# Routing arithmetic kept in tokens, and the order of all steps written out as a list, in a fused linear attention and mixture-of-experts kernel

## The chip, the cores and the metric

The kernel runs on one core of a Trainium2 chip. The metric is the device time of one execution in microseconds (us). Before the change the median of three runs is 667.26 us (663.68, 667.26 and 671.38). TensorE is called PE here, VectorE DVE, ScalarE ACT, GpSimd POOL and SyncE SP.

## The reference

Attention with random features over eight batches and eight heads gives 4608 rows of 512; each row then goes through one of eight experts, the one with the largest gate logit.

```python
# q, k, v: [8, 8, 576, 64]; omega: [128, 64]
def phi(x):
    proj = np.einsum('bhsd,md->bhsm', x, omega)
    h = proj - np.sum(x * x, axis=-1, keepdims=True) / 2.0
    h = h - np.max(h, axis=-1, keepdims=True)
    return np.exp(h) / np.sqrt(m)
q_p, k_p = phi(q_s), phi(k_s)                     # q, k scaled by 64 ** -0.25
kv = np.einsum('bhsm,bhsd->bhmd', k_p, v)
z = np.sum(k_p, axis=2)
num = np.einsum('bhsm,bhmd->bhsd', q_p, kv)
den = np.einsum('bhsm,bhm->bhs', q_p, z)[..., None] + 1e-06
x = (num / den) -> rows [4608, 512]

logits = x @ w_gate                               # [4608, 8]
e_idx = np.argmax(logits, axis=1)
gate_w = softmax(logits)[np.arange(N), e_idx]
eom = 1.0 / (1.0 + np.exp(-(x @ w_output_gate)))
for e in range(8):
    mask = e_idx == e
    h = np.maximum(x[mask] @ w1[e], 0.0)          # w1[e]: [512, 1024]
    out[mask] = gate_w[mask, None] * eom[mask, e, None] * (h @ w2[e])
```

## The kernel before

**Attention.** The work is cut into 32 units: four groups of tokens (nine chunks of 128 tokens each) by eight pieces of heads. A unit u goes through these steps, each named by its kind and its unit:

- SP loads k and q in two layouts (ld t, ld n) and v (ld v), ahead of time.
- ACT makes the f16 part of the transposed input (hi, tile xhi) and the squares (sqa, tile sqt, L442); POOL makes the remainder (lo, tile xlo, L436).
- PE multiplies by omega (pp, L502). DVE takes the maximum (L524) and makes the bias (nb, L537); ACT takes the exponential (ex, tile ef, L543).
- ACT casts ef to f16 (eh, tile es, L564), POOL makes the remainder beside it (el, L566). PE sums es times v (kv, L639), DVE scales the sum (kvs, L700).
- PE makes the gate products of the kv sums (kt, and kg at L682, in f32).
- For most units SP transposes es by a DMA from SBUF to SBUF (eT, tile et, L620); the first eight units are transposed on PE. PE multiplies et by kvs (pn, L713); DVE normalizes (tiles xf and xh), POOL makes the remainder xl (L747), and SP stores the rows to DRAM (rows).

Buffers limit how far units run apart: es, et and the input tiles have two each.

**Routing.** After the eight units of a group, DVE finds the expert of every token: route makes the one-hot r_one of the argmax; PE's counts multiplies it with a triangle of ones, which gives each token its place within its expert; ranks, places, table, assign and lists on DVE turn that into lists of 128 tokens; PE (pid) and DVE then give the indices gi. All this is a chain of small DVE instructions on a tile called rt, with 8 or 9 elements per partition in most. Experts are filled in blocks of 128 tokens: the arithmetic turns a count into blocks by a cast to int32, a shift by 7 and a cast back.

**Experts.** Item n is one block of up to 128 tokens of one expert. There are 49 slots in groups of 8, 8, 9 and 24; with these inputs 38 run. POOL gathers the rows (gx, L1446); SP transposes them (xt, L1458); PE multiplies by w1 (hA and hB, L1483, in f16 with a remainder w1l); ACT takes the relu (hh, L1490), DVE its remainder (rest, tile hl, L1494); PE multiplies by w2 (out, L1514; L1506 where at most 64 rows are filled); ACT scales the result (os, L1567); POOL scatters it (put, L1556). When the expert changes, SP brings the weights, ACT cuts them to f16 (sw, L364, w1h and w2h) and DVE makes the remainders (swl, L368). The items of group 0 stand among the units of the later groups; the items of the last group come after all units.

**The order of all this.** Every step is added to a `Plan` with its engine, a cost, what it follows, the tiles that it reads, and the PSUM banks that it takes and frees. `Plan.order` is a list scheduler: it picks, at each moment of a modelled time, the step with the lowest rank among those that could start now. The rank is a due time plus a number for the kind of step (`SHIFT`):

```python
s = dict(..., rank=(rank + SHIFT.get(key[0], 0.0), self.seq), bank=bank)
...
k = min((k for k in ready if steps[k]["est"] <= best + TIE), key=lambda k: steps[k]["rank"])
```

The steps are issued in the order that comes out, on each engine's queue; five banks are kept for one class of requests, three for another (`Plan({"a": 5, "b": 3})`). There are 3333 steps.

Of the kernel before, what the change touches and what calls it, by code (L numbers as in the profile page):

```python
# [21 lines left out]
P = 128  # L22
# [4 lines left out]
NSC = 4  # L27
# [4 lines left out]
KEY = 64  # L32
KC = DM // P
# [39 lines left out]
SHIFT = {'hi': -1.4, 'lo': 0.3, 'sqa': 1.9, 'sqr': 2.3, 'T': 1.8, 'pp': 0.1, 'mx': 0.5, 'nb': -0.4, 'ex': -2.0, 'eh': -0.7, 'el': 1.4, 'eT': 0.4, 'kv': -0.5, 'kvs': -1.6, 'pn': -0.1, 'xf': -0.9, 'xh': 0.1, 'xl': 0.7, 'xT': -3.4, 'rows': -0.1, 'lg': -2.2, 'lga': -1.4, 'route': -1.8, 'gx': 1.7, 'xt': 1.0, 'hA': 0.7, 'hB': -1.1, 'relu': -2.1, 'rest': -0.6, 'out': 0.3, 'os': -0.1, 'put': 1.0}  # L73
# [25 lines left out]
C_END = C_DOWN + 1  # L99


def constants():
# [6 lines left out]
    c[:, C_ITEM:C_PART] = np.arange(NITEM)  # L109
# [4 lines left out]
    c[FEW:, C_DOWN] = -float(FEW)  # L114
    c[:, C_BOTH + 1 : C_UPPER : 2] = np.arange(NSC * NC) * P
# [3 lines left out]
    m[:, 2, :] = np.arange(P)  # L119
    m[:, 3, :] = np.eye(P)  # L120
    return c, m, np.eye(P, dtype=np.float32)


class Plan:

    HANDOFF, DRAIN, DMA_START, DMA_END, DMA_TURN, BACKLOG, LATE = 0.19, 0.13, 0.65, 0.95, 0.3, 2.5, 2.5
    TICK, ENOUGH = 3.413, 3060.0

    def __init__(self, banks):
        self.steps, self.seq, self.banks, self.bank_of = {}, 0, banks, {}
        self.part = 0
        self.makers, self.readers, self.bufs = {}, {}, {}

    def add(
        self, key, engine, cost, fn, after=(), rank=0.0, tiles=(), bank=None, frees=(), dma=0.0, turn=False, early=None, cols=None,
        lead={},
    ):


        assert key not in self.steps, key
        cost = cost if isinstance(cost, tuple) else (cost,) * len(engine)
        bank = [] if bank is None else bank if isinstance(bank, list) else [bank]
        s = dict(key=key, eng=engine, cost=cost, fn=fn, after=list(after), rank=(rank + SHIFT.get(key[0], 0.0), self.seq), bank=bank)  # L150
        s.update(frees=frees, dma=dma, turn=turn, tiles=sorted(set(tiles)), early=early, part=self.part, lead=lead)
        s["cols"] = cost[0] * 2400.0 if cols is None else cols
        self.seq += 1
        self.steps[key] = s
        for tag, i in s["tiles"]:
            self.readers.setdefault((tag, i), []).append(key)
# [18 lines left out]
    def lag(self, a, b):  # L175

        if a == b:
            return 0.0 if a == ("PE",) else self.DRAIN
        return 0.06 if b == ("SP",) else self.HANDOFF

    def order(self):
        steps = self.steps
        users, missing = {}, {}
        for k, s in steps.items():
            deps = set(s["after"])
            for tag, i in s["tiles"]:
                deps |= set(self.readers.get((tag, i - self.bufs[tag]), ()))
            s["deps"] = deps
            missing[k] = len(deps)
            for d in deps:  # L190
                assert d in steps, (k, d)
                users.setdefault(d, []).append(k)
        free_at = {"SP": 0.6, "DVE": 0.9, "POOL": 0.7, "ACT": 1.9, "PE": 0.1}
        bank_free = {b: 0.0 for b in range(sum(self.banks.values()))}
        bank_cls, b0 = {}, 0
        for c, n in self.banks.items():
            bank_cls[c] = range(b0, b0 + n)
            b0 += n
        bank_cls["e"] = range(b0)
        dma_free = 0.0  # L200
        ready = {k for k in steps if not missing[k]}
        at = {k: 0.0 for k in ready}
        out, done = [], {}
        busy = {}
        while ready:
            best = None
            for k in ready:
                s = steps[k]
                engs = s["eng"]
                t = max([at[k]] + [free_at.get(e, 0.0) for e in engs])  # L210
                if s["bank"]:
                    free = sorted(bank_free[b] for b in bank_cls[s["bank"][0][0]] if b in bank_free)
                    t = max(t, free[len(s["bank"]) - 1] if len(free) >= len(s["bank"]) else 1e9)
                if s["dma"] and engs == ("SP",):
                    t = max(t, dma_free - self.BACKLOG)
                s["est"] = t
                if best is None or t < best:
                    best = t
            assert best < 1e9, sorted(ready, key=str)[:20]

            k = min((k for k in ready if steps[k]["est"] <= best + TIE), key=lambda k: steps[k]["rank"])
            s = steps[k]
            t = s["est"]
            ready.remove(k)
            for cls, name, _ in s["bank"]:
                b = min((b for b in bank_cls[cls] if b in bank_free), key=lambda b: bank_free[b])
                del bank_free[b]
                self.bank_of[name] = b
            if s["eng"] == ("PE",):

                end, left = t, s["cost"][0]
                while left > 1e-6:
                    tick = int(end / self.TICK + 1e-6)
                    speed = 1.0 if busy.get(tick - 1, 0.0) >= self.ENOUGH else 0.5
                    part = min(left, ((tick + 1) * self.TICK - end) * speed)
                    busy[tick] = busy.get(tick, 0.0) + s["cols"] * part / s["cost"][0]
                    end, left = end + part / speed, left - part
                free_at["PE"] = end
            else:
                end = t + max(s["cost"])  # L240
                for e, cost in zip(s["eng"], s["cost"]):
                    free_at[e] = t + cost
            for name in s["frees"]:
                bank_free[self.bank_of[name]] = end + self.HANDOFF
            fin = end if s["early"] is None else t + s["early"]
            if s["dma"]:
                b = max(end + self.DMA_START, dma_free)
                dma_free = b + s["dma"] + (self.DMA_TURN if s["turn"] else 0.0)

                fin = b + s["dma"] + self.DMA_END + (self.LATE if s["turn"] else 0.0)  # L250
            done[k] = fin
            s["t"] = (t, end, fin)
            out.append(s)
            for u in users.get(k, ()):
                missing[u] -= 1
                e = fin + self.lag(s["eng"], steps[u]["eng"]) - steps[u]["lead"].get(k, 0.0)
                at[u] = max(at.get(u, 0.0), e)
                if not missing[u]:
                    ready.add(u)
# [1398 lines left out]
```

## Time and profile before

| | |
|---|---|
| median of the three runs | 667.26 us (663.68 to 671.38) |
| profiled execution, its own time | 664.8 us |
| its span in the trace | 663.0 us |
| mean granted clock of PE | 0.961 of full speed |
| DMA moved | 129.09 MB |
| last product of PE ends | 649.8 us after the span's start |

The profile comes from one execution. Its page gives the busy time of each engine, in all and in 40 equal slices of the span as tenths, and below them the granted clock of PE. Rows of groups give one line, engine, operation and tile; the count after x, the busy time, the mean of one in ns, and the idle time ahead of them with the releaser that ended most of it. Rows of the timeline give start, duration, engine, line, operation, output tile <- input tiles, shapes, and in square brackets the wait ahead of the instruction and what ended it. In the waits of an engine the three numbers are the time in all, the count and the longest.

### The profile page before, as it was taken

Reading aid. Unit: us, or ns where it says so; the run is one execution under the profiler, and the core shown is the slowest. Engines: PE = TensorE matmul, PEld = TensorE weight load, DVE = VectorE, ACT = ScalarE, POOL = GpSimd, SP = SyncE. Lnnn points to the kernel's source line nnn. Section 1 sums busy time; section 2 is a strip of 40 time slices with the busy share of each in tenths; the row PEclk is TensorE's granted clock in tenths of the full one; section 3 lists DMA queues with packets and bytes.
Section 4 is the critical chain, followed back from the end, with each engine's and each line's share of the span. In section 5 each row is a group of like instructions: output and inputs, shape, how many; then the busy total and the mean of one; then the engine's idle time right before and its main releaser. Section 6 shows DMA issues by size and latency. Waiting matters only on the chain. (4 is left out here: it accounts for less than half of the span.)

```text
span 663.0 us, 22360 instructions
## 1 busy us (share of the span) xinstructions
PE 610.9 (92%) x8732; PEld 479.8 (72%) x8732; DVE 425.7 (64%) x1277; ACT 413.0 (62%) x970; POOL 340.5 (51%) x235
## 2 busy tenths in 40 slices
PE   6999987799999899999788999999999899999972
PEld 6899976677777677777555777878677767676761
DVE  4899889876978897576587776753882611431160
ACT  5876887589989759898575588762611611521150
POOL 1342445569957958989376588965031312131110
PEclk9999977699999999999899999999999999999996
DMA  9544578997999979999999675877747647642730
GB/s 317 207 136 129 174 281 197 254 252 167 319 275 287 272 191 221 227 225 235 277 257 170 149 194 126 144 134 198 226 113 211 183 92 234 172 90 62 268 112 8
DMA packets 145895, 129.09 MB, mean 195 GB/s; under 512 B 104271, under 2 KB 127441, under 8 KB 144465
## 3 DMA queue, kind: packets, MB, share of 16 engines
q1 hardware_dynamic: 139760, 107.45, 64.0%
q0 software_dynamic: 5984, 19.72, 9.4%
q8 instruction: 85, 1.39, 0.9%
q14 instruction: 66, 0.53, 0.3%
HBM read 83.86 MB, written 19.30 MB: 156 GB/s over the span
## 5 line engine op out<-in xcount | busy, mean ns | idle before, releaser
L1483 PE MATMUL ph<-xt,w1h 128*128 128x128 f16 (+1 forms) x2432 | 205.2, 218 | 3.4 <-ACT os L1567 1.6
L1483 PE MATMUL ph<-xt,w1l 128*128 128x128 f16 (+1 forms) x1216 | 201.3, 218 | 0.0
L1483 PEld LDWEIGHTS <-w1h 128*128 128x128 f16 x2432 | 181.9, 98 | 10.8 <-issue 4.4
L543 ACT ACTIVATE ef<-pp,nb 128x128 f32<-128x128 f32 x576 | 162.8, 392 | 41.5 <-DVE nb L537 31.6
L1494 DVE SCALAR_TENSOR_TENSOR hl<-ph,hh 128x512 f16<-128x512 f32 (+1 forms) x76 | 50.6, 666 | 116.4 <-ACTq L1412 76.6
L566 POOL TENSOR_TENSOR es<-ef,es 128x1152 f16<-128x1152 f32 x44 | 104.9, 2391 | 35.6 <-ACT es L564 19.5
L524 DVE TENSOR_REDUCE pp<-pp 128x3 f32<-128x384 f32 x192 | 102.8, 557 | 28.2 <-PE pp L502 27.7
L1483 PEld LDWEIGHTS <-w1l 128*128 128x128 f16 x1216 | 118.5, 98 | 0.3 <-DVEq L1407 0.2
L1446 POOL DMA_INDIRECT gx<-rows,gi x38 | 40.8, 1074 | 140.5 <-ACT os L1567 100.6
L1514 PE MATMUL po<-w2h,hl 128*128 128x512 f16 x280 | 107.0, 382 | 2.4 <-DVEq L1412 1.5
L1514 PE MATMUL po<-w2h,hh 128*128 128x512 f16 x280 | 107.4, 384 | 0.0
L1514 PE MATMUL po<-w2l,hh 128*128 128x512 f16 x280 | 107.1, 383 | 0.0
L1490 ACT ACTIVATE hh<-ph 128x512 f16<-128x512 f32 (+1 forms) x76 | 44.3, 583 | 80.0 <-PE ph L1483 73.6
L1514 PEld LDWEIGHTS <-hh 128*128 128x128 f16 x560 | 51.9, 99 | 58.0 <-issue 3.7
L1567 ACT ACTIVATE os<-po,gx 128x512 f32<-128x512 f32 (+1 forms) x38 | 25.5, 670 | 72.9 <-PE po L1514 68.0
L436 POOL TENSOR_TENSOR xlo<-xt,xhi 128x1152 f16<-128x1152 f32 x24 | 57.2, 2382 | 13.2 <-ACT xhi L429 12.7
L713 PE MATMUL pn<-kvs,et 128*128 128x81 f16 (+1 forms) x960 | 48.2, 210 | 12.3 <-DMA et<-es 7.2
L713 PEld LDWEIGHTS <-et 128*128 128x128 f16 (+1 forms) x960 | 41.6, 105 | 21.2 <-DMA et<-es 7.9
L564 ACT CAST es<-ef 128x1152 f16<-128x1152 f32 x44 | 51.3, 1176 | 7.4 <-DMA et<-es 6.9
L1514 PEld LDWEIGHTS <-hl 128*128 128x128 f16 x280 | 27.6, 99 | 35.3 <-DVE hl L1494 1.3
L502 PE MATMUL pp<-omh,xhi 64*128 64x128 f16 x432 | 43.0, 223 | 5.0 <-DVE xf L726 2.7
L747 POOL TENSOR_TENSOR xs<-xf,xs 128x576 f16<-128x576 f32 x32 | 42.1, 1317 | 8.9 <-DVE xs L743 8.1
(183 smaller groups left out, 1052.8 us busy)
## 6 DMA issues: line engine op xcount, KB each, us to landing
r<-w SPq DMA_DIRECT2D x10, 2048.0 KB, 11.9
xt<-kqt SPq DMA_DIRECT2D x32, 576.0 KB, 4.7
xn<-kqn SPq DMA_DIRECT2D x24, 576.0 KB, 4.9
rawv<-v SPq DMA_DIRECT2D x32, 325.0 KB, 3.7
rows<-xs SPq DMA_DIRECT2D x16, 576.0 KB, 5.3
r<-w SPq DMA_DIRECT2D x8, 512.0 KB, 6.6
ef<-w SPq DMA_DIRECT2D x2, 512.0 KB, 4.4
et<-w SPq DMA_DIRECT2D x2, 512.0 KB
```

The costliest lines, as they stand in the source:

```text
L436: lambda t0=t0, t1=t1: nc.gpsimd.tensor_tensor(out=xl(u)[:, t0:t1], in0=xt32(u)[:, t0:t1], in1=xh(u)[:, t0:t1], op=ALU.subtract),
L502: nc.tensor.matmul(banks["pp", 2 * u + i, g][:, c, :], x[r, t], w[r, :], start=(a == 0), stop=(a == len(ops) - 1))
L524: nc.vector.tensor_reduce(out=pp[:, 3, 0:3], in_=pp[:, 0:3, :], op=ALU.min, axis=AX.X)
L543: nc.scalar.activation(ef(n)[:, c, :], banks["pp", n, g][:, c % 3, :], AF.Exp, bias=nb(n)[:, c : c + 1], scale=-SK)
L564: nc.scalar.copy(es(slot_es(n))[:, 0], ef(n))
L566: nc.gpsimd.tensor_tensor(out=es(slot_es(n))[:, 1], in0=ef(n), in1=es(slot_es(n))[:, 0], op=ALU.subtract)
L713: nc.tensor.matmul(pn[lo:hi, c - c0, :], a[:, c, lo:hi], w[:, b, :], start=(i == 0), stop=(i == len(ops) - 1))
L747: nc.gpsimd.tensor_tensor(out=x[:, :, P + o : P + o + D], in0=xf(u)[:, :, 0:D], in1=x[:, :, o : o + D], op=ALU.subtract)
L1483: nc.tensor.matmul(ph[:, f4, 0:w_], w[qd][:, kk, fo : fo + P], xt(n)[:, x, 0:w_], start=(a == 0), stop=(a == 3 * KC - 1))
L1490: nc.scalar.activation(hh(n)[:, sl, 0:w_], banks["ph", n, g][:, :, 0:w_], AF.Relu)
L1494: nc.vector.scalar_tensor_tensor(out=hl(n)[:, sl, 0:w_], in0=banks["ph", n, g][:, :, 0:w_], scalar=0.0, in1=hh(n)[:, sl, 0:w_], op0=ALU.ma ...
L1514: nc.tensor.matmul(po, x(n)[:, f, :], w[f // 2][:, f % 2, :], start=(f == 0 and a == 0), stop=(f == FC - 1 and a == 2))
```

## The change

Two things are changed.

**First, the routing keeps its counts in tokens.** The state `cnt` and `done`, the item numbers and the block starts are multiples of 128 where they were block numbers. A count is rounded to whole blocks by adding a constant ROUND, 1.5 x 2^23 x 128, and taking it off again: at that size an f32 has steps of 128. A count is held lower by 63.5 so that this rounds down. The running count is added by PE: counts begins its two sums with a product of the f32 identity and `cnt`. The steps fall from 9 to 7 in table (8 in the last group), from 8 to 7 in assign, from 4 to 3 in ranks, from 5 to 3 in places; the copy of the chunk numbers (cp) moves from lists to places in the first three groups. In all 23 DVE steps fewer, six in each of groups 0 to 2 and five in group 3, and eight PE products more.

**Second, the order is written out.** `Plan` has no scheduler any more. `ORDER` lists the numbers of all 3310 steps (numbered as they are added), and `BANKS` has one digit for each request of a bank; any of the eight banks may serve any request.

```diff
+MIDDLE = (P - 1) / 2
+ROUND = 1.5 * 2.0**23 * P
...
+ORDER = """
+0 31 32 4 86 3 7 33 5 35 34 36 16 1 2 28 88 37 6 39 40 48 49 41 50 8 38 42 43 51 52 54 45 55 57 89 44 53 56 10 139 19
...
+BANKS = """
+0123456701235467150234671234507631276415702361546734052671364127056341263471652037120476153472365031042635612702067431
...
     def order(self):
...
+        numbered = list(self.steps.values())
+        out = [numbered[int(x)] for x in ORDER.split()]
...
-    plan = Plan({"a": 5, "b": 3})
+    plan = Plan()
...
     def first_state():
-        nc.vector.tensor_scalar(cnt, eidx, float(KEY * P), None, ALU.mult)
-        nc.vector.tensor_scalar(done[:, 0, :], eidx, float(KEY), None, ALU.mult)
-        nc.vector.tensor_copy(done[:, 1, :], eidx)
+        nc.vector.tensor_scalar(cnt, eidx, float(KEY * P), -MIDDLE, ALU.mult, ALU.add)
+        nc.vector.tensor_scalar(done, eidx, float(KEY * P), ROUND, ALU.mult, ALU.add)
...
     def counts(j):
...
-        nc.tensor.matmul(pos[:, 0:NC, :], tri, one, start=True, stop=False)
+        nc.tensor.matmul(pos[:, 0:NC, :], ident, cnt.unsqueeze(1).broadcast_to([P, NC, NE]), start=True, stop=False)
+        nc.tensor.matmul(pos[:, 0:NC, :], tri, one, start=False, stop=False)
...
+        nc.tensor.matmul(pos[:, NC, :], ident, cnt, start=True, stop=False)
         for c in range(NC):
-            nc.tensor.matmul(pos[:, NC, :], ones, one[:, c, :], start=(c == 0), stop=(c == NC - 1))
+            nc.tensor.matmul(pos[:, NC, :], ones, one[:, c, :], start=False, stop=(c == NC - 1))
 
     def ranks(j):
...
-        nc.vector.tensor_tensor(
-            out=pk, in0=pos[:, 0:NC, :], in1=cnt.unsqueeze(1).broadcast_to([P, NC, NE]), op=ALU.add
-        )
-        yield
-        nc.vector.tensor_tensor(out=cnt, in0=cnt, in1=pos[:, NC, :], op=ALU.add)
-        yield
-        nc.vector.tensor_tensor(out=pk, in0=pk, in1=rt[j]["one"], op=ALU.mult)
+        nc.vector.tensor_tensor(out=pk, in0=pos[:, 0:NC, :], in1=rt[j]["one"], op=ALU.mult)
+        yield
+        nc.vector.tensor_copy(cnt, pos[:, NC, :])
...
     def places(j):
...
-        nc.vector.tensor_copy(ri, rank)
-        yield
-        nc.vector.tensor_scalar(ri, ri, 7, None, ALU.arith_shift_right)
-        yield
-        nc.vector.tensor_copy(key, ri)
-        yield
-        nc.vector.scalar_tensor_tensor(out=rank, in0=key, scalar=-float(P), in1=rank, op0=ALU.mult, op1=ALU.add)
+        nc.vector.tensor_scalar(key, rank, ROUND, ROUND, ALU.add, ALU.subtract)
+        yield
+        nc.vector.tensor_tensor(out=rank, in0=rank, in1=key, op=ALU.subtract)
...
     def table(g):
...
-        nc.vector.tensor_scalar(av_i, cnt, float(P - 1) if g == NG - 1 else 0.0, None, ALU.add)
-        yield
-        nc.vector.tensor_scalar(av_i, av_i, 7, None, ALU.arith_shift_right)
...
-        nc.vector.tensor_tensor(out=av, in0=av_i, in1=done[:, 0, :], op=ALU.subtract)
...
-        nc.vector.tensor_tensor(out=t["av"], in0=av_i, in1=done[:, 0, :], op=ALU.subtract)
+            for x in (av, t["av"]):
+                nc.vector.scalar_tensor_tensor(out=x, in0=cnt, scalar=ROUND, in1=done, op0=ALU.add, op1=ALU.subtract)
```

The lists differ from what the scheduler gave in many places: 84 of PE's 502 steps, 692 of DVE's, 341 of ACT's, 104 of POOL's and 144 of SP's stand elsewhere. Three places follow. In them L922 to L958 of the kernel before are L979 to L1021 of the changed one; in general the line numbers of the changed kernel are some 56 to 60 higher.

On DVE, in the routing of group 0, places (writing keys) and table (writing r_avs) run side by side, with pieces of the next units (nb, pp) between. Before:

```order
L922 CAST rt_1670<-rt_1670 128x9
L947 TENSOR_SCALAR rt_1670<-cnt 128x8
L537 SCALAR_TENSOR_TENSOR nb_1783<-pp_0_1561,sqs_1553 128x3
L924 TENSOR_SCALAR rt_1670<-rt_1670 128x9
L949 TENSOR_SCALAR rt_1670<-rt_1670 128x8
L926 CAST keys<-rt_1670 128x9
L952 TENSOR_TENSOR rt_1670<-rt_1670,done 128x8
L928 SCALAR_TENSOR_TENSOR rt_1670<-keys,rt_1670 128x9
L955 TENSOR_TENSOR r_avs<-rt_1670,done 128x8
L930 TENSOR_TENSOR place<-cmt,rt_1670 128x1152
L958 TENSOR_TENSOR rt_1670<-ahead,rt_1670 128x64
```

The same place of the changed kernel:

```order
L1012 SCALAR_TENSOR_TENSOR rt_1656<-cnt,done 128x8
L1012 SCALAR_TENSOR_TENSOR r_avs<-cnt,done 128x8
L590 SCALAR_TENSOR_TENSOR pp_1_1671<-pp_1_1671,sqs_1512 128x3
L979 COPY rt_1656<-cft 128x18
L1015 TENSOR_TENSOR rt_1656<-ahead,rt_1656 128x64
L594 SCALAR_TENSOR_TENSOR nb_1780<-pp_1_1671,sqs_1512 128x3
L581 TENSOR_REDUCE pp_2_1691<-pp_2_1691 128x3
L1018 TENSOR_REDUCE r_tot<-rt_1656 128x1
L981 TENSOR_SCALAR keys<-rt_1656 128x9
L1021 TENSOR_REDUCE rt_1656<-rt_1656 128x8
L590 SCALAR_TENSOR_TENSOR pp_2_1691<-pp_2_1691,sqs_1512 128x3
L983 TENSOR_TENSOR rt_1656<-rt_1656,keys 128x9
```

The four steps of table up to r_avs have become two, the chunk copy stands here, and table now runs ahead of places, whose wide product (place, 128x1152) comes later.

On ACT, between the squares of a later unit (sqt) and the relu of item 11 (hh), stand the f16 cast of unit 23 (es, which needs an es buffer that the et transfer of unit 21 must have read) and the cutting of item 12's w1 (w1h, inside a branch that is taken only when the expert changes). Before:

```order
L442 ACTIVATE sqt_7209<-xn_6621 128x1152
L564 CAST es_7216<-ef_6867 128x1152
L1407 COMPARE_AND_BRANCH
L364 ACTIVATE w1h_90<-r_106 128x1024
L364 ACTIVATE w1h_91<-r_106 128x1024
L364 ACTIVATE w1h_92<-r_106 128x1024
L364 ACTIVATE w1h_93<-r_106 128x1024
L1407 UNCONDITIONAL_BRANCH x2
L1392 UNCONDITIONAL_BRANCH
L1490 ACTIVATE hh_7154<-ph_1_7156 128x512
```

The same place of the changed kernel:

```order
L499 ACTIVATE sqt_7175<-xn_6534 128x1152
L600 ACTIVATE ef_7093<-pp_1_7100,nb_7085 128x128 x3
L1463 COMPARE_AND_BRANCH
L421 ACTIVATE w1h_90<-r_106 128x1024
L421 ACTIVATE w1h_91<-r_106 128x1024
L421 ACTIVATE w1h_92<-r_106 128x1024
L421 ACTIVATE w1h_93<-r_106 128x1024
L1463 UNCONDITIONAL_BRANCH x2
L1448 UNCONDITIONAL_BRANCH
L621 CAST es_7198<-ef_6839 128x1152
L1546 ACTIVATE hh_7122<-ph_1_7126 128x512
```

The cutting of w1 now stands ahead of the cast, with three exponentials of a later unit ahead of both. On PE at the same place the order was hB 11, both halves of pn 22 (which waits for et), out 11 and hA 12; it is now hB 11, out 11, half of kv 23, both halves of pn 22 and hA 12. On ACT the cutting of item 12's w2 moves ahead of the scaling (os) of item 11 and of the copy of kv (kvf).

On POOL, in the time of group 1's counts, the remainder el of unit 17 (es from ef), the subtraction lo of unit 19 (xlo) and the remainder xl of unit 15 (xs) stand in turn. Before:

```order
L566 TENSOR_TENSOR es_4524<-ef_4016,es_4524 128x1152
L1392 UNCONDITIONAL_BRANCH
L587 TENSOR_TENSOR vs_4415<-rawv_4058,vs_4415 128x650
L436 TENSOR_TENSOR xlo_4678<-xt_4076,xhi_4512 128x1152
L747 TENSOR_TENSOR xs_4284<-xf_4592,xs_4284 128x9x64
L566 TENSOR_TENSOR es_4680<-ef_4421,es_4680 128x1152
```

The same place of the changed kernel:

```order
L623 TENSOR_TENSOR es_4479<-ef_3914,es_4479 128x1152
L1448 UNCONDITIONAL_BRANCH x2
L1463 UNCONDITIONAL_BRANCH
L1448 UNCONDITIONAL_BRANCH
L623 TENSOR_TENSOR es_4652<-ef_4373,es_4652 128x1152
L804 TENSOR_TENSOR xs_4381<-xf_4571,xs_4381 128x9x64
L493 TENSOR_TENSOR xlo_4752<-xt_4051,xhi_4484 128x1152
```

The remainder of unit 17 has moved from the last of the three to the first. On PE the order there was counts 1, kt 16, hA 6, kg 16 and the two halves of kv 17; it is now counts 1, kt 16, both halves of kv 17, kg 16 and hA 6. Item 6 has no dependence on these.

Four more moves bear on what follows. POOL gathered for items 0, 1 and 2 in that order at the end of group 0's routing, and now gathers for 2, 1 and 0, with a subtraction (lo 12) and a gate sum between. SP issued the transposes xt 0, 1 and 2 ahead of the input load of unit 15 (ld n 15), and now issues xt 0 behind it. At the start of the kernel SP loads omega first and the first input second, the other way round than before. At the last item, 37, DVE makes the remainder hl ahead of the fourth w2 cut, where it stood behind it.

More of the change, by code (lines that the diff above doesn't have):

```diff
@@ L98 @@
 C_DOWN = C_UPPER + 1
-C_END = C_DOWN + 1
+C_LANE = C_DOWN + 1
+C_END = C_LANE + 1
 def constants():
```

205 lines of the change are left out of this document (70 added, 135 removed), and 133 rows, old and new, of the table ORDER.

## The prediction

> **What bounds the kernel now.** I read the page first, for the engine that is busy when the others are not.
>
> ```profile
> span 663.0 us, 22360 instructions
> ...
> PE 610.9 (92%) x8732; PEld 479.8 (72%) x8732; DVE 425.7 (64%) x1277; ACT 413.0 (62%) x970; POOL 340.5 (51%) x235
> ...
> PE   6999987799999899999788999999999899999972
> PEclk9999977699999999999899999999999999999996
> ```
>
> TensorE is the bound nearly everywhere: 92% busy, and in the slices where it is not, the granted clock falls as well. So only two things are for sale: time in which PE stands still, and time in which it works at half clock. The rest of the DVE, ACT and POOL time is hidden. The waits of PE name the stills:
>
> ```profile
> PE pn L713 <- DMA et<-es: 7.2, 2, 4.1
> PE pn L713 <- DVE kvs L700: 2.1, 2, 1.8
> PE ph L1483 <- ACT os L1567: 1.6, 2, 1.4
> ```
>
> The windows below (busy time of PE, PEld, DVE, ACT, POOL, then the clock) follow the clock's own steps of about 3.4 us:
>
> ```profile
> 89.20:92.60 3.40, 2.23 (x44) 1.62 (x38) 3.33 (x13) 3.40 (x9) 1.74 (x2) 1.00 0.60 175
> 92.60:99.40 6.80, 5.93 (x44) 5.70 (x46) 5.06 (x18) 5.37 (x19) 2.70 (x2) 0.50 0.74 261
> 96.00:122.00 26.00, 19.02 (x229) 16.25 (x228) 21.41 (x105) 15.03 (x42) 15.29 (x10) 0.63 0.85 210
> 225.70:229.10 3.40, 1.85 (x41) 1.75 (x41) 2.91 (x16) 2.90 (x11) 2.91 (x2) 1.00 0.94 289
> 229.10:232.50 3.40, 3.40 (x35) 3.40 (x33) 3.06 (x12) 0.95 (x2) 3.39 (x3) 0.51 1.06 346
> 321.30:324.70 3.40, 3.40 (x34) 2.36 (x35) 1.24 (x1) 3.38 (x4) 2.10 (x1) 0.50 1.21 403
> ```
>
> A step in which PE worked 2.23 or 1.85 of 3.40 us is followed by a step at clock 0.5. A wait therefore costs its own length and, where it thins out such a step, up to 1.7 us more (half of the next 3.4). From 96 to 122, the routing of the first group of tokens, DVE is busy 21.41 of 26 us and PE only 19.02 at a mean clock of 0.63: that stretch alone belongs to DVE.
>
> The Trainium skill states it otherwise: TensorE: Matmul & The Clock Gate, section "Why this matters for your kernels", advises no PE idle gaps over about 3 us, since one idle window brings half clock. By that rule the drop at 229.1 needs another cause than gaps of about 1 us, and the 1.7 us counted for it below would not come back, which makes my sum 657.7. The two windows at 89.2 and 225.7 speak against it: both were more than half busy.
>
> **The steps that go.** Groups 0 to 2 lose six DVE steps each (one in ranks, two in places, two in table, one in assign; the copy of chunk numbers only moves from lists to places), group 3 five: 23 in all.
>
> ```profile
> 104.79 0.17 DVE L947 TENSOR_SCALAR rt<-cnt 128x8 int32<-128x8 f32 x1
> 104.86 0.15 DVE L537 SCALAR_TENSOR_TENSOR nb<-pp,sqs 128x3 f32<-128x3 f32 x1
> 104.99 0.17 DVE L924 TENSOR_SCALAR rt<-rt 128x9 int32<-128x9 int32 x1
> ```
>
> A small step that needs nothing just made starts 0.07 us after the one before it (104.79, 104.86); the chained ones stand about 0.2 apart. So six steps are worth 0.4 to 1.2 us. In groups 1 to 3 PE has items to compute meanwhile, so I count nothing there. In group 0, where DVE is the bound, I take the upper end, nearest to the chained rows: **-1.0 us**. What is late next caps it:
>
> ```profile
> 122.29 4.12 SPq L1458 DMA_TRANSPOSE xt<-gx  x3
> 126.51 0.53 SPq L461 DMA_DIRECT2D xn<-kqn  x1
> 133.02 0.27 PE L1483 MATMUL ph<-xt,w1h 128*128 128x128 f16 x2
> ...
> xt<-gx SPq DMA_TRANSPOSE x38, 3.9
> ```
>
> Item 0 starts on PE at 133.02. Its transpose xt 0 was issued at 122.29, ahead of the xn load at 126.51. In the new order POOL gathers for items 2, 1, 0, with a subtraction and a sum between, and SP puts the same xn load (of unit 15, which waits until ACT has read unit 13's) ahead of xt 0. So xt 0 goes out at about 127 instead of 122.3 and, with the 3.9 us that a transpose of this kind takes to land, is there at 131. PE can hardly start item 0 earlier, which leaves at most 2 us to be won here.
>
> **The steps that are added.** Each group's counts gains two f32 products with the identity. The nearest row is the other small f32 product:
>
> ```profile
> L682 PE MATMUL kv<-wgr,kvf 128*128 128x32 f32 x64 | 12.2, 274 | 1.3 <-ACT kvf L688 1.3
> ```
>
> Those are 32 products (two records each), 0.38 us apiece, so eight cost at most 3.0 us. The lower end is 0: the first of each pair needs no new data and stands ahead of the one that waits for r_one. I take half: **+1.5 us**.
>
> **The steps that move: unit 22.** PE's longest wait is here.
>
> ```profile
> 314.14 1.18 ACT L442 ACTIVATE sqt<-xn 128x1152 f32<-128x1152 f32 x1
> 321.32 1.15 ACT L564 CAST es<-ef 128x1152 f16<-128x1152 f32 x1 [6.00 <-DMA et<-es]
> 322.38 3.89 ACT L364 ACTIVATE w1h<-r 128x1024 f16<-128x1024 f32 x4
> ...
> 321.29 2.29 PE L713 MATMUL pn<-kvs,et 128*128 128x81 f16 x30 [4.14 <-DMA et<-es]
> 325.12 0.38 PE L1514 MATMUL po<-w2h,hl 128*128 128x512 f16 x1
> 325.34 0.38 PE L1514 MATMUL po<-w2h,hh 128*128 128x512 f16 x1
> ```
>
> PE waits 4.14 us for the transposed et of unit 22, and ACT 6.00 us for the same transfer, with the cutting of w1 (322.38) and then a relu queued behind. Now PE does out 11 0 first (12 products, 0.22 apart by the two rows: 2.6 us) and half of kv 23 (0.5, half of the kv row of the next part), and ACT cuts w1 ahead of the cast. Of 4.14 us, 3.1 are filled. hA 12 needs the cut w1; it can begin when PE has left w1, at 321.29 - 4.14 = 317.15, takes 3.89 and DVE's last piece 1.2 more, so it is ready at about 322.3, when PE is through pn. SP issues the transfer where it did, behind the first half of item 12's weights. **-3.0**, and the half-clock step after it, **-1.7**. The cover is out 11 0; if its hl is late, all 3 us are back.
>
> **Group 1.** hA 6 waits for an output tile to be emptied:
>
> ```profile
> 228.09 0.27 PE L1483 MATMUL ph<-xt,w1h 128*128 128x128 f16 x2 [1.37 <-ACT os L1567]
> 232.59 1.09 PE L639 MATMUL kv<-vs,es 128*128 128x65 f16 x30
> 221.17 2.39 POOL L436 TENSOR_TENSOR xlo<-xt,xhi 128x1152 f16<-128x1152 f32 x1
> 225.46 2.37 POOL L566 TENSOR_TENSOR es<-ef,es 128x1152 f16<-128x1152 f32 x1
> ```
>
> kv 17 (1.09 us) moves from behind hA 6 to ahead of it. It needs the es made at 225.46 to 227.83, too late to fill anything; but POOL now makes this es ahead of the 2.39 us subtraction of 221.17, so it is there 2.4 us earlier, by about 225.4, and PE has finished counts and kt at 228.09 - 1.37 = 226.7. **-1.1**, and the clock step at 229.1, **-1.7**.
>
> **Item 12's w2, and the end.**
>
> ```profile
> 334.75 0.70 ACT L1567 ACTIVATE os<-po,gx 128x512 f32<-128x512 f32 x1
> 335.47 3.93 ACT L364 ACTIVATE w2h<-r 128x1024 f16<-128x1024 f32 x4
> ...
> 641.65 3.49 DVE L368 SCALAR_TENSOR_TENSOR w2l<-r,w2h 128x1024 f16<-128x1024 f32 x3
> 645.05 0.42 DVE L1494 SCALAR_TENSOR_TENSOR hl<-ph,hh 128x256 f16<-128x256 f32 x1
> 645.53 0.41 PE L1506 MATMUL po<-w2h,hl 128*64 128x256 f16 x2 [1.50 <-DVE hl L1494]
> ```
>
> The w2 cut of item 12, behind which DVE's kvs L700 stands, moves ahead of os 11 and kvf: 0.8 of that kvs wait of 1.8 goes, **-0.8**. At the last item, hl (645.05) stands behind four w2 cuts; now only three stand ahead of it, and the rows give a cut 1.16 us (3.49 for three): I take **-1.0** of PE's 1.50.
>
> All other moves (the first loads, swapped nb, ex and half cuts, stores of rows that SP issues later but still ahead of the gathers that read them) lie where PE was busy or waits for something that did not move; I count them 0, between -4.8 (the second et wait, 7.2 - 4.1 = 3.1, and its clock step) and what the third rival costs.
>
> **Sum:** -1.0 + 1.5 - 3.0 - 1.7 - 1.1 - 1.7 - 0.8 - 1.0 = -8.8. The profiled execution took 664.8 us, 1.8 more than its span, and 2.5 below the median of the runs shown (667.26). 664.8 - 8.8 = **656.0 us**, which I keep as the forecast.
>
> **The rivals.** *The et loop takes the gain back.* There are two es buffers, so the cast at 321.32 waits for one et to land and the next et is issued only after it:
>
> ```profile
> 305.95 10.23 SPq L620 DMA_TRANSPOSE et<-es  x1
> 325.00 5.26 SPq L620 DMA_TRANSPOSE et<-es  x1
> 347.55 4.08 SPq L620 DMA_TRANSPOSE et<-es  x1
> ...
> 361.39 0.40 PE L713 MATMUL pn<-kvs,et 128*128 128x81 f16 x6 [3.10 <-DMA et<-es]
> ```
>
> Issues stand 19 to 22.5 us apart. If the DMA sets that pace, PE meets the saved 5.5 us (3.0 + 1.7 + 0.8) again as a longer wait two units on: 661.5. Against it: the issue at 347.55 followed casts that had waited for ACT's w2 cut. *The clock comes back in group 0.* In 96 to 122 it lost up to 0.37 x 26 = 9.6 us; with 4.8 for the second et wait at most 14.4, at half that 649. Against it: the cap at item 0. *Slower: item 0 waits.* Place: xt 0 behind the xn load on SP. It decides when xt 0 lands after 133. If its transfer is as slow as the et issued at 347.55, for which PE was held until 361.39, 13.8 us, it lands near 140: 7 us of still PE, two clock steps lost (3.4) and the -1.0 gone, 667.4, slower than the 664.8 before; with the next et queued behind it on SP delayed as much, up to 675. Against it: such slow landings stand where weights are loaded too, and none are here. *It does not act:* the filled waits reopen at the next step and only the -0.8 stays: 664.0.
>
> **How the numbers follow.** Forecast 0.42, loop 0.22, clock 0.17, item 0 0.12, no effect 0.07. The range for 8 in 10 goes from 642 (most of the clock case) to 670 (most of the slower case). About 1% is what the measurement can tell from no change, so faster means under 660.6 and slower over 673.9. Faster: nearly all of the forecast (0.40), the clock case, a little of the loop (0.04): 0.61. Slower: the far end of the item 0 case and a rest: 0.09. Within: 0.30.
>
> **What would show it.** Right: no PE wait of 4 us for et near 317, no clock step at 0.5 near 229 and 321, DVE with 23 fewer steps, the wait for hl at the end near 0.5. Wrong: a wait of ph at item 0 on xt; the second wait for et grown to 7 us or more; new half-clock steps in 133 to 300, where there is one now.

## The result, and the profile after

The changed kernel takes 688.95 us in the median of four runs (685.41 to 696.35), against 665.47 us (660.29 to 671.38) for the kernel before on the same chip: a ratio of 1.0362, 95% interval 1.0256 to 1.0468. It is slower, by about 23 us, where 656 was forecast. Medians here and below are over all runs, while ratios leave out slow runs, those over 1.5% above the fastest of their kernel (here 696.35 and 671.38), so a ratio is not the quotient of two medians.

The page of the changed kernel, the rows that answer to those shown of before:

```profile
span 685.8 us, 22340 instructions
...
PE 613.3 (89%) x8748; PEld 477.6 (70%) x8748; DVE 428.6 (63%) x1253; ACT 414.4 (60%) x970; POOL 339.6 (50%) x235
...
PE   6999975899899997979989999999999899999960
PEclk9999997799999998999999999999999999999995
```

PE's busy time grew by 2.4 us (613.3 against 610.9); the granted clock is no worse (0.965 against 0.961 on average). The span grew by 22.8 us, so nearly all of it is time in which PE stands still. The waits of PE name where:

```profile
PE pn L770 <- DMA et<-es: 7.1, 3, 3.1
PE ph L1539 <- issue: 5.5, 5, 1.8
...
PE kv L696 <- POOL es L623: 4.0, 2, 3.6
PE ph L1539 <- DVE w1l L425: 3.5, 3, 1.9
```

The wait for kvs at pn has fallen from 2.1 to 1.8 in all with a longest of 0.6, but new waits for es, w1l and "issue" (nothing that the profile shows) have come.

The next table cuts the span where PE begins an item (64 products with w1h belong to each, so the start of every 64th is an item's start). "Old order" is the first experiment, profiled in two executions.

| us | before | after | old order, new arithmetic | the same, again |
|---|---|---|---|---|
| to item 0 | 133.0 | 135.5 | 131.1 | 133.4 |
| item 0 to 5 | 77.1 | 83.9 | 77.1 | 77.0 |
| item 5 to 10 | 85.0 | 94.1 | 87.4 | 88.0 |
| item 10 to 15 | 88.2 | 81.8 | 86.5 | 80.4 |
| item 15 to 20 | 76.1 | 78.5 | 76.1 | 76.1 |
| item 20 to 26 | 65.2 | 65.8 | 66.9 | 66.0 |
| item 26 to 33 | 76.1 | 80.6 | 78.4 | 77.1 |
| item 33 to PE's last product | 49.1 | 49.3 | 48.3 | 48.7 |
| after it | 13.2 | 16.2 | 13.0 | 12.8 |

The stretch with unit 22 (items 10 to 15) did get shorter, by 6.4. The other eight all got longer, by 29.2 together. One of their waits reads like this. POOL, then PE, in the changed kernel around 260 us:

```profile
252.86 1.02 POOL L1612 DMA_INDIRECT out<-os,oi  x1 [0.30 <-ACT ef L600]
254.19 0.99 POOL L1502 DMA_INDIRECT gx<-rows,gi  x1 [0.30 <-issue]
255.17 0.33 POOL L820 COPY lga<-xf 128x144 f32<-128x144 f32 x1
259.67 1.02 POOL L1612 DMA_INDIRECT out<-os,oi  x1 [4.18 <-DMA out<-os,oi]
260.71 4.70 POOL L623 TENSOR_TENSOR es<-ef,es 128x1152 f16<-128x1152 f32 x2
...
263.15 1.06 PE L696 MATMUL kv<-vs,es 128*128 128x65 f16 x16 [3.60 <-POOL es L623]
```

The first scatter of results (put 6, at 252.86) lands at 259.40. The second (put 5), which stands only two instructions (gx 9 and lga 16) behind it in the new list, waits 4.18 us for that, since both write the same output. The remainders es of unit 18 stand behind it on POOL, and PE stands still 3.60 us for them. The granted clock is then 0.5 from 262.0 to 268.8. The kernel before has its scatters 12 to 20 us apart here and no such wait.

### The profile page after: what moved, and what is told of

Same layout as the page of the kernel before. It is cut to its first block, busy times and chain, and to the rows that moved or that the text cites. A ratio compares the mean times of both kernels' runs of the same rounds, so it can differ in the third digit from the quotient of the medians.

```text
span 685.8 us, 22340 instructions
## 1 busy us (share of the span) xinstructions
PE 613.3 (89%) x8748; PEld 477.6 (70%) x8748; DVE 428.6 (63%) x1253; ACT 414.4 (60%) x970; POOL 339.6 (50%) x235
## 5 line engine op out<-in xcount | busy, mean ns | idle before, releaser
L600 ACT ACTIVATE ef<-pp,nb 128x128 f32<-128x128 f32 x576 | 165.1, 388 | 49.0 <-DVE nb L594 26.1
L581 DVE TENSOR_REDUCE pp<-pp 128x3 f32<-128x384 f32 x192 | 104.2, 557 | 23.3 <-PE pp L559 21.5
L1546 ACT ACTIVATE hh<-ph 128x512 f16<-128x512 f32 (+1 forms) x76 | 44.8, 589 | 78.5 <-PE ph L1539 73.5
L770 PE MATMUL pn<-kvs,et 128*128 128x81 f16 (+1 forms) x960 | 46.4, 205 | 9.1 <-DMA et<-es 7.1
L770 PEld LDWEIGHTS <-et 128*128 128x128 f16 (+1 forms) x960 | 39.9, 102 | 17.5 <-DMA et<-es 8.3
```

The source lines that it names most:

```text
L581: nc.vector.tensor_reduce(out=pp[:, 3, 0:3], in_=pp[:, 0:3, :], op=ALU.min, axis=AX.X)
L600: nc.scalar.activation(ef(n)[:, c, :], banks["pp", n, g][:, c % 3, :], AF.Exp, bias=nb(n)[:, c : c + 1], scale=-SK)
L770: nc.tensor.matmul(pn[lo:hi, c - c0, :], a[:, c, lo:hi], w[:, b, :], start=(i == 0), stop=(i == len(ops) - 1))
L1546: nc.scalar.activation(hh(n)[:, sl, 0:w_], banks["ph", n, g][:, :, 0:w_], AF.Relu)
```

## The experiments

In all of them the kernel is the changed one with another list, so its line numbers hold. They are numbered in the order in which they were made. Ratios are to the kernel before on the same chip, whose median was 659.5 to 662.2 us in these comparisons. Where a list joins stretches of both orders (runs 6, 7, 9, 11 and 12), the banks could not all stay: 46, 9 and 279 of the 472 requests have another bank in runs 6, 11 and 12 than in run 1, and 39 in runs 7 and 9 than in the changed kernel.

**Old order, new arithmetic.** The 23 steps that went are dropped from the scheduler's list; order and banks stay.

```diff
-ORDER = the new list
+ORDER = the scheduler's order of before, without the steps that went
```

> The changed kernel's arithmetic (23 DVE steps fewer, eight f32 products more), with all steps in the order and the banks that the scheduler gave before; the steps that went are simply left out of the list. Theory A (the order costs the time, the arithmetic next to nothing): within 0.5% of the kernel before, 662 to 668 us. Rival B (the arithmetic costs it: the added f32 products hold up counts, or the rounding steps are slower than those they replace): 680 us or more.

Measured (run 1): 666.89 us, 1.0133 (1.0069 to 1.0197). The time lies in the range of theory A, but the ratio is not within 0.5%, so the same kernel was run more often, on another chip:

> The first run's kernel again, against the kernel before. If the arithmetic costs time, the ratio comes out again at 1.007 to 1.02; if the first ratio came of a spread between runs of the kernel before (655 to 668 us there), it comes out within 0.995 to 1.006.

Measured (run 8, twelve executions): 661.47 us, 1.0004 (0.9970 to 1.0038). Here the arithmetic is neutral; the order costs the time. Why the first ratio was 1.3% higher stays unexplained, so ratios of different comparisons can't be told apart to better than about 1%. The two profiles of this one kernel also differ by 5.4 us of span, and most of that is one wait. PE's waits from 300 to 350 us, first in the one, then in the other:

```profile
PE pn L770 <- DMA et<-es: 5.2, 1, 5.2
PE pn L770 <- DMA rawv<-v: 1.6, 1, 1.6
```

```profile
PE pn L770 <- DVE kvs L757: 1.8, 1, 1.8
PE pp L559 <- DVE xf L783: 1.1, 1, 1.1
```

The wait for et at unit 22, on which the largest terms of the forecast rested, is 5.2 us in one execution and absent in the next.

**The scatters, in the changed kernel.** POOL's queue, shorthand by step and item or unit. El 26 and el 27 make the remainders es of unit 13, vl makes the remainder of v, lga sums for the gates, gx gathers, put scatters:

```diff
-el 26, put 0, vl 14, put 1, gx 4, el 27
+put 0, xl 11, el 25, vl 13, lo 15, lga 11, el 26, vl 14, gx 4, put 1, el 27
...
-gx 8, put 6, gx 9, lga 16, put 5, el 36, el 37
+put 5, el 35, vl 19, vl 18, lo 20, xl 16, gx 8, gx 9, put 6, lga 16, el 36, el 37
```

> The changed kernel with one thing altered in its list: the 38 scatters of results (put) go back to item order on POOL, none nearer than about 6.5 us to the last one among the units, and put 36 ahead of put 37. Theory A1 (a scatter waits until the scatter before it has landed, and POOL's remainders el stand behind it, so that PE waits for es and et at 180 and 260): -3.0 and -1.7 at et of unit 13, -3.6 and -1.7 to -3.4 at es of unit 18, -3.1 at the end, so 673 to 678 us against the changed kernel's 688. Rival A2 (SP's order, loads ahead of the transposes, makes et late): these waits stay or move, only the -3.1 at the end comes, 684 us or more.

Measured (run 2): 685.48 us, 1.0398 (1.0325 to 1.0470), above the 673 to 678 us of theory A1. This run had drawn new banks too, so it was made again with the list's own:

> As the second run (the changed kernel's list with the scatters in item order and apart), but with the banks as the changed kernel has them; the second run had drawn new banks for all requests, by the order in which they come free in the list, and in its trace PE waits 2.87 and 1.92 us in new places (pp for hl). Theory A1 (the near scatters cost et of unit 13, es of unit 18 and the end): -11 to -13 us against the changed kernel, so 1.5 to 2.2% over the kernel before on the same chip, and the stretch from item 5 to item 10 falls from 94 to about 87 us. Rival A2 (the scatters' places are not what costs): 3% or more over the kernel before.

Measured (run 5): 689.06 us, 1.0438 (1.0380 to 1.0497), so the forecast of the sum failed. In its profile items 0 to 5 take 79.9 us (83.9 after) and the waits at 180 and 260 are gone, but items 5 to 10 still take 94.1. PE's waits from 140 to 310:

```profile
PE pn L770 <- DMA et<-es: 7.3, 2, 5.7
```

The wait for et at unit 20, 3.1 us after, is now 5.7: the time freed at unit 18 was taken back there. Items 15 to 33, whose scatters this edit moves too, take 231.5 us where they took 224.9 after; that takes back another 6.6, for a reason that was not looked for.

**The last scatters.** The new list has put 37 ahead of put 36.

```diff
-put 35, put 37, put 36
+put 35, put 36, put 37
```

> The changed kernel with put 36 and put 37 exchanged in the list, nothing else. Theory A1: put 36 starts when os 36 is done, near 664 us of the span, and the time after PE's last product falls from 16.2 to about 13.2 us, the span by 3.1. Rival (the end is set by something else than the scatters): the time after the last product stays at 16.

Measured (run 3, one execution): 690.37 us. Scaling (os) and scatters of items 36 and 37, first after, then here:

```profile
663.04 0.46 ACT L1623 ACTIVATE os<-po,gx 128x256 f32<-128x256 f32 x1
...
670.39 0.98 POOL L1612 DMA_INDIRECT out<-os,r_oi  x1 [14.91 <-ACT os L1623]
673.45 0.98 POOL L1612 DMA_INDIRECT out<-os,r_oi  x1 [2.07 <-ACTq L1658]
```

```profile
669.28 0.45 ACT L1623 ACTIVATE os<-po,gx 128x256 f32<-128x256 f32 x1
...
670.01 1.10 POOL L1612 DMA_INDIRECT out<-os,r_oi  x1 [8.46 <-ACT hh L1546]
676.00 0.98 POOL L1612 DMA_INDIRECT out<-os,r_oi  x1 [4.89 <-ACT os L1623]
```

After, os 36 is done at 663.5, but its scatter goes out at 673.45, behind that of item 37. Exchanged, it follows os 36 at once, and the time after PE's last product falls from 16.2 to 13.4 us, as forecast. The whole was no shorter, since this execution lost 5.6 us elsewhere before its last product.

**The near scatters alone, in the old order.**

```diff
-put 0, lga 11, xl 11, el 25, vl 13, lo 15, el 26, vl 14, el 27, gx 4, put 1
+lga 11, xl 11, el 25, vl 13, lo 15, el 26, put 0, vl 14, put 1, gx 4, el 27
```

> The kernel of the first run (old order, new arithmetic) with the scatters of items 0 to 11 where the changed kernel's list has them on POOL (put 0 and put 1 with one step between, both ahead of el of unit 13; put 3, a gather, put 2; put 6 ahead of put 5), nothing else. Theory A1: POOL stands still 2 to 5 us at the second put of each of the three pairs, and PE meets part of it: 4 to 12 us more than the first run. Rival A2 (puts do not matter): no more than 2 us of difference.

Measured (run 4): 673.06 us, 1.0225 (1.0163 to 1.0286), 6.2 us over the first run beside it. POOL's second scatter and the remainder behind it, then PE's waits:

```profile
160.17 1.02 POOL L1612 DMA_INDIRECT out<-os,oi  x1
...
168.56 1.02 POOL L1612 DMA_INDIRECT out<-os,oi  x1 [5.90 <-DMA out<-os,oi]
169.88 0.99 POOL L1502 DMA_INDIRECT gx<-rows,gi  x1 [0.30 <-issue]
170.90 2.39 POOL L623 TENSOR_TENSOR es<-ef,es 128x1152 f16<-128x1152 f32 x1
```

```profile
PE kv L696 <- POOL es L623: 5.0, 1, 5.0
PE pn L770 <- DMA et<-es: 4.4, 3, 3.0
```

Both waits of the changed kernel, at unit 13 and at unit 18, appear in the old order by this edit alone: items 0 to 10 take 9.4 us longer than in the first run's profile (items 10 to 15 take 3.2 less, with 0.9 us of waiting for et at unit 22 instead of 5.2).

**The late order, taken out and put in.** As an example, ACT's cuts of item 34's weights (swh 34 1 3 is the cut of the last quarter of its w1):

```diff
-swh 34 1 3, swh 34 1 2, swh 34 1 0, swh 34 1 1, relu 33 1, os 33
+swh 34 1 0, swh 34 1 1, relu 33 1, swh 34 1 2, swh 34 1 3, ..., os 33
```

> The fifth run's kernel with the old order from item 15 on. Theory (of the changed kernel's loss some 12 us are the scatters and some 7 us the order of the late items: cuts of weights split and reordered on ACT and DVE, one w1l wait with a clock step at item 27): 6 to 9 us under the fifth run, 0.3 to 1.2% over the kernel before. Rival (the late loss is chance in instruction waits, which the trace calls issue): no more than 3 us under the fifth run.

Measured (run 7): 679.69 us, 1.0281 (1.0223 to 1.0339), 9.4 under the fifth run, but not the 0.3 to 1.2% over the kernel before that were forecast. Part of what is left stands where the two orders meet: items 15 to 20 take 82.8 us, where the old order has 76.1. Two scatters are 5.3 us apart there (at 391.01 and 396.29), and the second waits 1.64 us for the first.

> The old order with the new arithmetic up to item 18, the changed kernel's list from there on (weight cuts split up and put in another order on ACT and DVE, scatters out of order, put 37 ahead of put 36). Theory D (the late order costs by itself): item 26 to item 33 takes 80 us or more where the old order has 75.8 to 78.4, the time after PE's last product is 16 us where it was 13, the whole 5 to 9 us over the old order. Rival (chance in instruction waits): only the 3 us at the end.

Measured (run 11): 675.06 us, 1.0226 (1.0137 to 1.0315), which is more than the forecast 5 to 9 us over the old order. PE's waits from 450 us on, first with the late order, then in the old one:

```profile
PE ph L1539 <- issue: 6.8, 6, 1.7
PE ph L1539 <- DMA xt<-gx: 3.3, 2, 1.7
PE ph L1539 <- DVE w1l L425: 3.1, 2, 2.5
```

```profile
PE ph L1539 <- issue: 4.1, 5, 1.5
PE po L1562 <- DVE hl L1550: 2.6, 2, 1.5
```

The remainders w1l come 2.5 us late at item 26 (27 in the forecast), and the transposes xt of two items come 1.6 and 1.7 us late; items 26 to 33 take 81.8 us (77.1 and 78.4 in the old order) and the end 17.3. So the late order costs by itself. "Issue" waits stand in both; they differ between executions, and their cause stays open.

**SP's burst, taken out and put in.** SP's queue between et 19 and et 20 (ld n, t and v are loads of a unit's input; bring loads an item's w1 or w2 when the expert changes). Of the two edits the first reaches from et 17 to et 22, the second from et 17 to et 21:

```diff
-eT 19, ld v 22, ld t 24, bring 9 2, xt 9, bring 10 1, ld n 26, ld t 23, xt 10, ld n 27, eT 20
+xt 9, ld n 25, bring 9 1, eT 18, ld t 23, bring 9 2, ld n 26, xt 10, eT 19, bring 10 1, ld v 22, ld t 24, ld n 27, ld v 23, bring 10 2, eT 20
```

> The seventh run's kernel (scatters apart, old order from item 15 on) with SP's queue between et of unit 17 and et of unit 22 in the old order as well. There the changed kernel's list has between et 19 and et 20 four input loads and the transposes xt 9 and xt 10, which stood behind et 19 while it waited for POOL; et 20 comes last of the burst and in the seventh run PE waited 6.72 us for it, with a half-clock stretch of 6.8. Theory C (SP's burst is what the freed time turned into): that wait goes, the stretch from item 5 to item 10 falls from 94 to 86 or 87 us, and the whole is 6 to 9 us under the seventh run, 1.4 to 2% over the kernel before. Rival (et 20 is late since its es is late): the wait stays over 3 us.

> The old order with the new arithmetic, and SP's queue between et of unit 17 and et of unit 21 as in the changed kernel, nothing else. Theory C: a wait of 3 to 7 us for et at unit 20 with a half-clock stretch, the stretch from item 5 to item 10 at 92 to 97 us where the old order has 87 to 88, and the whole 5 to 9 us over the old order. Rival (the burst hurts only where POOL is late): within 2 us of the old order.

The first (run 9): 675.73 us, 1.0233 (1.0148 to 1.0318), not the 1.4 to 2% that were forecast; the wait for et of unit 20 falls from 6.7 to 1.6 and the half-clock step goes, but items 5 to 10 still take 92.6 us, where 86 or 87 were forecast, now in several waits, none over 1.7. That remainder was not taken apart. The burst alone in the old order (run 10): 673.91 us, 1.0167 (1.0084 to 1.0249), items 5 to 10 at 94.9, as forecast, and the whole somewhat over the forecast 5 to 9 us; its profile also has the wait at unit 22, with 5.4 us. SP's queue with the burst, and PE behind it:

```profile
269.29 2.75 SPq L677 DMA_TRANSPOSE et<-es  x1
272.13 0.53 SPq L522 DMA_DIRECT2D rawv<-v  x1
273.00 0.33 SPq L518 DMA_DIRECT2D xt<-kqt  x1
273.76 1.85 SPq L1514 DMA_TRANSPOSE xt<-gx  x1
275.99 0.34 SPq L518 DMA_DIRECT2D xn<-kqn  x1
276.38 0.44 SPq L518 DMA_DIRECT2D xt<-kqt  x1
276.93 2.18 SPq L1514 DMA_TRANSPOSE xt<-gx  x1
279.21 0.54 SPq L518 DMA_DIRECT2D xn<-kqn  x1
281.34 7.07 SPq L677 DMA_TRANSPOSE et<-es  x1
...
295.74 0.97 PE L770 MATMUL pn<-kvs,et 128*128 128x81 f16 x18 [4.16 <-DMA et<-es]
```

The transposes xt 9 and xt 10 and five loads (the forecast said four) stand behind et 19; once it is out they follow within 8 us, and the et of unit 20, last in the line, takes 14 us from its issue to the product.

**The start.** The new list up to item 0, the old one behind it.

> The changed kernel's list up to item 0 (the first loads, group 0's units and routing, the gathers of items 2, 1 and 0), the old order from there on, new arithmetic. Theory E (the start costs by itself): item 0 begins at 134 to 136 us where the old order has 130.4 to 133.4, the whole 2 to 4 us over the old order. Rival (no difference outside the spread of 130 to 133): within 1 us.

Measured (run 12): 670.91 us, 1.0104 (0.9987 to 1.0221). Item 0 begins at 136.5. PE's waits from 85 to 150:

```profile
PE pp L559 <- DVE done L1181: 3.3, 1, 3.3
PE pp L559 <- DVE rt L1015: 2.9, 1, 2.9
PE ph L1539 <- DMA xt<-gx: 2.8, 1, 2.8
```

PE's pp, whose banks DVE has to free, waits twice for instructions of the routing chain, which the new list has moved forward on DVE; the third row is the prediction's slower rival, item 0 waiting for xt 0, in 2.8 us. The first two are not the work of the new banks: they are 3.3 and 2.6 us in the ninth run, which has mostly the changed kernel's banks. In seven profiles with the new start item 0 begins at 134.0 to 136.5, in ten with the old one at 130.0 to 135.6, so the new start is later by some 3 us on the average, but the ranges overlap.

**The forecast's own moves.** First the new list for items 10 to 15 alone:

> The first run's kernel (old order, new arithmetic) with the changed kernel's list for the stretch from item 10 to item 15 alone (unit 22, the cutting of item 12's weights, the et issues there). Theory of the prediction (the wait for et at unit 22, its clock step and the wait for kvs behind item 12's w2 are filled): the stretch from item 10 to item 15 takes 81 to 82 us where it took 86.5, and the whole is 4 to 6 us under the first run. Rival (the et loop, or waits that stood before, take it back): within 1.5 us of the first run.

Measured (run 6): 667.56 us, 1.0123 (1.0063 to 1.0183), no shorter than the first run. Items 10 to 15 take 81.7, as forecast, but items 15 to 20 take 81.7 where 76.1 was: the seam had brought a near pair of scatters (POOL waits 4.65 us at 387.05 for the one at 380.08). So the named moves were made by themselves (eh 47 is the cast es of unit 23, sw 12 1 and sw 12 2 are the cuts of item 12's w1 and w2, ke 23 is the copy kvf):

```diff
-PE: hB 11, pn 22 0, pn 22 5, out 11 0, hA 12, kv 23 0
+PE: hB 11, out 11 0, kv 23 0, pn 22 0, pn 22 5, hA 12
-ACT: eh 47, sw 12 1, relu 11 1 ... os 11, ke 23, sw 12 2
+ACT: sw 12 1, eh 47, relu 11 1 ... sw 12 2, os 11, ke 23
```

> The old order with the new arithmetic, and of the changed kernel's moves only the four that the prediction named at unit 22: PE does out 11 0 and half of kv 23 ahead of pn 22, ACT cuts item 12's w1 ahead of the cast eh 47 and its w2 ahead of os 11 and ke 23. Theory F (the wait for et at unit 22 comes in about half of the executions, so the moves are worth about half of the forecast 5.5 us on average): the stretch from item 10 to item 15 takes 80 to 82.5 us in its profile, and the median is 2 to 3 us under the old order, 0.994 to 0.998 of the kernel before. Rival (the prediction's full term): 5 us or more, 0.992 or less. Rival (the et loop takes it back): no difference, 1.000 or more.

Measured (run 13): 663.93 us, 1.0044 (1.0006 to 1.0082): no gain, though its profile has no wait for et there and items 10 to 15 at 80.2.

```diff
-PE: counts 1, kt 16, hA 6, kg 16, kv 17 0, kv 17 1
+PE: counts 1, kt 16, kv 17 0, kv 17 1, kg 16, hA 6
-POOL: lo 19, xl 15, el 34
+POOL: el 34, lo 19, xl 15
```

> The old order with the new arithmetic, and of the changed kernel's moves only those that the prediction named in group 1: PE does kv 17 ahead of kg 16 and hA 6, POOL makes the remainder el 34 ahead of lo 19 and xl 15. Theory of the prediction: the wait of 1.15 us at hA 6 and the half-clock step of 3.4 us behind it, which stand in every profile of the old order so far, both go: 2 to 3 us less, 0.995 to 0.998 of the kernel before. Rival (lo 19 and xl 15, now later, hold up pp or rows): no gain, 1.000 or more.

Measured (run 14): 659.11 us, 0.9966 (0.9926 to 1.0005). Windows of 3.4 us there (busy PE, PEld, DVE, ACT, POOL, then the clock), first the old order, where they are the clock's own steps:

```profile
225.50:228.90 3.40, 1.57 (x28) 1.33 (x27) 3.12 (x16) 1.77 (x7) 3.24 (x2) 1.00 1.08 337
228.90:232.30 3.40, 3.29 (x32) 3.28 (x32) 3.12 (x8) 2.04 (x6) 3.04 (x3) 0.50 1.08 349
```

```profile
224.00:227.40 3.40, 3.40 (x47) 2.31 (x46) 2.75 (x14) 3.13 (x10) 3.40 (x2) 1.00 0.92 215
227.40:230.80 3.40, 3.40 (x74) 3.40 (x71) 3.09 (x12) 1.85 (x5) 3.24 (x4) 1.00 0.47 149
```

PE is busy throughout and the step at 0.5 is gone; items 5 to 10 take 83.9 us (87.4 and 88.0).

> The moves of the last two runs together. If they add up: 4 to 6 us under the kernel before, 0.991 to 0.994 of it, and faster than either kernel of this study. If one step's freed time is taken back at the next wait: no better than the better of the two.

Measured (run 15): 660.76 us, 0.9951 (0.9908 to 0.9994). The forecast of 4 to 6 us is not reached: the ratio lies half a per cent under the kernel before, with an interval that just stays below 1, and the median is the same as beside it (660.78). So a gain over the kernel before is not shown. The unit 22 moves add nothing that can be told to the group 1 moves, and in this profile PE waits 2.9 us at unit 24 for DVE's routing of group 2.

## Why the prediction was wrong

**The step that failed: "All other moves ... I count them 0".** That clause took in SP's loads, the weight cuts, the start and the scatters, the last without naming them; for a loss only item 0 had a price, in the third rival. Put in alone, against the old order with the same arithmetic, they cost: near scatters 6.2 us, SP's burst 1.6%, the late order 2.2%, the start 1.0% with an interval that includes no change. The first was measured beside the first run; the other three are set against the eighth run, made at another time, so their sizes are uncertain by about 1% of the time, and it is their profiles that show the loss: 7 us in items 5 to 10 for the burst, some 4 us each in items 26 to 33 and at the end for the late order. The reason given, that they "lie where PE was busy or waits for something that did not move", was not looked up queue by queue: I had followed PE and ACT to the places where PE waited, not POOL and SP to the instructions behind the ones that now wait. The sum of the parts is more than the 3.6% of the whole, and taken out of the changed kernel the scatters brought nothing: at unit 20 the fifth run shows a freed wait reopening at the next place. That this holds for the rest of the difference is not shown. Of the prediction's signs of being wrong one came: half-clock steps at 183.5 and 262.0 us, where before 229.1 was the only one between 133 and 300.

**Unit 22, -3.0 and -1.7: the mechanism was right, the wait was no fixed property.** The new order filled it (items 10 to 15 fall by 6.4 us after). But of the eight profiles with the old order at that place (before, and runs 1, 4, 8, 10, 11, 12 and 14) three have a wait of 4.1 to 5.4 us for this et, one 0.9 and four none. One execution's longest wait was taken for the kernel's, and the moves alone brought nothing (1.0044).

**Group 1, -1.1 and -1.7: right in the trace.** The wait at hA 6 (0.4 to 1.4 us) stands in all nine profiles with the old order there, its clock step in all but those of runs 4 and 10, so the step does not always follow; both go with the moves: 3.5 to 4.1 us in the stretch, 0.3% in the time, whose interval just reaches no change.

**Item 12's w2, -0.8, and the last hl, -1.0: came, and were lost.** After, the longest wait for kvs at pn is 0.6 (1.8 before), and the last item waits for no hl (1.5 before). But it waits 1.1 us that the trace calls "issue", the stretch from item 33 to the last product is no shorter, and behind it put 37 stands ahead of put 36, 3 us.

**Steps gone and products added, -1.0 and +1.5: right in sum.** The arithmetic as a whole is 1.0004, with an interval of some 2.5 us to either side; the two terms were not measured apart.

**The rivals.** The slower rival had the right side and a wait that does occur (2.8 us in the twelfth run), but in the changed kernel's own profile item 0 does not wait for xt, and it gave 3 to 10 us where 23 came. The et loop had a later et wait right in kind, but it came at unit 20, not 24, and by the loads and transposes that SP issues ahead of this et (runs 9 and 10), not by the pace of two es buffers. As for the clock in group 0: the half clock before item 0 lasted 17.1 us after, against 27.3 before, but also 13.7 and 20.5 in the two profiles of the old order with the new arithmetic, so this varies between executions, and item 0 began no earlier for it (135.5 against 133.0). As for the Trainium skill's rule on idle gaps that I set against the trace (TensorE: Matmul & The Clock Gate, section "Why this matters for your kernels"), the trace goes on to disagree: in the old order's rows above a step with 1.57 us of work, broken by waits of 0.8 and 1.15 us, is followed by one at 0.5.

## What to carry over

When an order changes everywhere, do not price the places where the bottleneck engine waits and count the rest at nothing: for every queue, go to each instruction that can wait, and ask what stands behind it. Scatters to one tensor, or any transfers that a program makes wait for each other, need a distance of a landing time (2.3 to 8.2 us for the scatters of the changed kernel), and an order made without regard to it may place them side by side. And before a long DMA wait is sold, see it in a second execution.

## What the runs showed of the hardware

The clock went with how busy PE was in the step of 3.41 us before. Over all the profiles here, without the first 12 and the last 20 us of PE's work, every one of 86 steps at full clock that was followed by a step at 0.5 had PE busy for at most 2.48 us; every one of the 86 steps at 0.5 that was followed by full clock had it busy for at least 2.91 us. Steps as thin as 1.45 us also stayed at full clock, and steps at 0.5 with up to 3.05 us of work stayed there, so a thin step was needed for a drop, and a well filled one for the return, but neither was enough.

Executions of one kernel on one chip spread by some 12 us (655.8 to 667.4 in seventeen runs of the kernel before; on another chip two of its twenty-nine took 771.8 and 1001.6, the others 654.8 to 665.7), and in the two profiles of one kernel the stretch with the wait for one transposing DMA, at unit 22, differs by 6.1.
